# Spreading the last batch finishes, moving the table scatter, and a reordered opening in a fused attention and top-1 MoE kernel

## The chip, the core and the metric

The kernel runs on one core of a Trainium2 chip. The metric is the device time of one execution in microseconds. The engines are TensorE (PE, with its weight loads as PEld), VectorE (DVE), ScalarE (ACT), GpSimd (POOL) and SyncE (SP), which here only issues DMAs. DMAs are issued from SP's queue and, where an index list is needed, from POOL's.

## What is computed

Eight batches of block-causal attention (8 heads, 576 tokens, 64 columns per head), whose output x goes through a top-1 mixture of 8 experts:

```
scores = scale * q @ k.T            # masked where block(i) < block(j), block = 64 tokens
attn   = softmax(scores);  x = attn @ v          # x: 4608 rows of 512
logits = x @ w_gate;  e = argmax(logits);  gate_w = softmax(logits)[e]
eom    = sigmoid(x @ w_output_gate)
out    = gate_w * eom[e] * (relu(x @ w1[e]) @ w2[e])      # for the rows of each expert
```

## The kernel before

**Attention.** The work is done in 32 pairs of heads, p = 0 to 31, four pairs per batch. A pair has 8 turns: `PLAN` (line 310) is a list of names, a `|` ends a turn. S0 to S4 are the score matmuls of five query tiles, M the maxima on DVE, E the exponentials on ACT, F and C the transposes of the probabilities (PE) and their copies out of PSUM (ACT), V and X the product with v of an earlier pair. So a pair's scores, its transposes and its product lie in three consecutive pairs, and two pairs (p = 32 and 33) follow the last scores. From p = 1 to 31 the orders of PE, DVE and ACT are those of the program; POOL's and SP's orders are a planner's, which follows the program's priorities. Pair 0 has a list of its own, `OPENING`, and there only PE's order is the program's.

**Loads.** `Load` (lines 85 to 121) brings k and q of four heads (one unit, two pairs): `split` makes an fp16 high part and a low part, in eight pieces for a unit; on POOL the pieces are paced by ACT (`behind`); `turn` issues the DMA transposes on SP, and `swap` on DVE copies the transposed k with its halves exchanged. `load_heads` (line 126) puts the eight pieces on eight successive turns, then the transposes and swaps. `load_start` (line 149) is the opening: the first unit in two halves, transposed by PE against an identity, and the second unit.

**Finish of a batch.** `finish_steps` (line 515) returns a list of steps, one for each turn, from the second pair of the following batch: logits, their transposes and scaling, `heads` (the sum over the heads), `choose` (the expert), `ranks`, `own`, `slots`, `shares`, `gather`, `gate`, `weights`, `scatter`, and for each of five row tiles a transpose T (PE) and a store K (DVE, then a DMA to `x_d`). `pace` selects the list: 1 has 32 steps (batches 0 to 4), 2 has 16 (batches 5 and 6), 3 has 12 (batch 7, behind the attention). With pace 1 `heads` and two small products run on POOL, else on DVE. The scatter is five indirect DMAs on POOL's queue, one per row tile.

**Experts.** At p = 28 `load_first` (line 923) chooses the fullest expert by the counts of batches 0 to 5, fetches the ids and x rows of the first tiles (POOL's queue, behind all scatters so far), loads that expert's w1 and w2 and splits them on POOL: `split_slowly` one quarter of a chunk per turn, then w2. `first_tiles` (line 1167) transposes those x rows on PE from p = 33 on. After batch 7's finish `route_rest` (line 747) works out the table of tiles on DVE, and the rest of the expert stage follows; there PE multiplies the tiles in the order of `run` (line 1213).

The list for pace 1, with the scatter in the thirty-first of 32 places:

```
[lge], [ke, lgb], [kb, recips], [turn_logits], [scale_logits], [turn_last], [scale_last], [heads],
[], [], [T(0)], [K(0)], [], [choose], [], [],
[], [T(1), ranks], [own, K(1), T(2)], [K(2)], [T(3), slots], [shares], [K(3)], [],
[], [], [T(4)], [K(4)], [gather], [gate], [weights, scatter], [],
```

Of the kernel before, what the change touches and what calls it, by code (L numbers as in the profile page):

```python
# [27 lines left out]
def block_attention_top1_moe(  # L28
# [120 lines left out]
    def load_start():  # L149
# [15 lines left out]
        def halves(i, which, hi, lo):  # L165
            nat, sp = nats[which][:, i], sps[which][:, i]
            hi(sp[:, :, 0, :], nat)
            lo.tensor_tensor(sp[:, :, 1, :], nat, sp[:, :, 0, :], ALU.subtract)

        halves(0, 0, nc.vector.tensor_copy, nc.vector)  # L170
        halves(0, 1, nc.scalar.copy, nc.vector)
        rest = ps_t.tile([P, 512], F32, name="ps_t").rearrange("p (a n) -> p a n", n=P)
        for i, (sp, tr) in enumerate(((sps[0], kT), (sps[1], qT), (sps[0], sw))):
            sp = sp[:, 0]
            tv = tr[:, 0:half].rearrange("c (r p) -> c r p", r=nr)
            ps = ps_s.tile([P, 2, 512], F32, name="ps_s").rearrange("p a (b n) -> p (a b) n", n=P)
            for r in range(nr):
                o = ps[:, r] if r < 8 else rest[:, i]
                if i == 2:
                    for c in range(2):  # L180
                        nc.tensor.matmul(o[64 * c:64 * c + 64], sp[:, r, 1 - c, :], ident16, start=True, stop=True)
                else:
                    nc.tensor.matmul(o, sp[:, r].rearrange("p c d -> p (c d)"), ident16, start=True, stop=True)
            nc.vector.tensor_copy(tv[:, 0:4], ps[:, 0:4])
            nc.scalar.copy(tv[:, 4:8], ps[:, 4:8])
            nc.vector.tensor_copy(tv[:, 8], rest[:, i])
        loaded[0] = (qT, kT, sw)
        for which in range(2):
            halves(1, which, nc.scalar.copy, nc.gpsimd)
# [5 lines left out]
        def turned(groups):  # L195
            for grp in groups:
                ps = ps_t.tile([P, 512], F32, name="ps_t").rearrange("p (a n) -> p a n", n=P)
                for i, (m, r) in enumerate(grp):
                    sp = sps[1 if m == 1 else 0][:, 1]
                    if m == 2:  # L200
                        for c in range(2):
                            nc.tensor.matmul(ps[64 * c:64 * c + 64, i], sp[:, r, 1 - c, :], ident16, start=True, stop=True)
                    else:
                        nc.tensor.matmul(ps[:, i], sp[:, r].rearrange("p c d -> p (c d)"), ident16, start=True, stop=True)
                i = 0
                while i < len(grp):
                    m, r = grp[i]
                    n = sum(1 for mm, _ in grp if mm == m)
                    tr = trs[m][:, half:] if m == 2 else trs[m][:, nr:].rearrange("c r p -> c (r p)")
                    nc.any.tensor_copy(tr.rearrange("c (r p) -> c r p", p=P)[:, r:r + n], ps[:, i:i + n])  # L210
# [5 lines left out]
        turned([[(2, r) for r in range(4)], [(m, 8) for m in range(3)]])  # L216
        nxt.turn(0)
        yield
        turned([[(0, r) for r in range(4, 8)], [(1, r) for r in range(4, 8)]])
        yield  # L220
        turned([[(2, r) for r in range(4, 8)]])
        with tc.issue_after(last_max[0].ins):
            nxt.split(1, nc.vector.tensor_copy, nc.gpsimd)
# [8 lines left out]

    with tc.high_priority(offset=3000):
# [4 lines left out]

        mrow = const.tile([P, P], BF16, name="mrow")
# [26 lines left out]
        nc.vector.tensor_copy(tcol, t_i)  # L266
        nc.vector.tensor_scalar(erev, ecol, -1.0, float(E), ALU.mult, ALU.add)

        nc.vector.tensor_tensor(
            upto, ecol.unsqueeze(2).broadcast_to([P, E, E]), ecol.unsqueeze(1).broadcast_to([P, E, E]), ALU.is_ge  # L270
        )

        nc.vector.tensor_scalar(t64, tcol, 64.0, None, ALU.mult)

# [20 lines left out]
    def constants():  # L295

# [218 lines left out]
    def finish_steps(b, sums, xT, pace):  # L515
# [16 lines left out]
        eng = nc.gpsimd if pace == 1 else nc.vector  # L532
# [95 lines left out]

        def slots():
            rank = small.tile([P, NT], F32, name="rank")  # L630
            nc.vector.tensor_reduce(rank, rk, AX.X, ALU.add)
            add = small.tile([P, E], F32, name="add")
            nc.vector.tensor_reduce(add, oh.rearrange("p t e -> p e t"), AX.X, ALU.add)
            nc.vector.tensor_tensor(run_cnt[:, b + 1], run_cnt[:, b], add, ALU.add)
# [288 lines left out]
    def load_first():  # L923
# [23 lines left out]
        for r in range(5):  # L947
            yield
# [348 lines left out]
```

## Time and profile before

| what | us |
|---|---|
| median of 3 runs | 763.81 (761.55 to 764.34) |
| the profiled execution | 760.33 |
| its span, first to last instruction | 758.4 |
| PE busy in the span | 724.5 |
| ACT busy | 532.1 |
| DVE busy | 525.5 |
| POOL busy | 341.5 |

The times in the rows below are microseconds from the start of the span. A row of a timeline gives start, duration, engine, line, operation, output and inputs, how many instructions it stands for, and in brackets the idle time of the engine ahead of it with what ended it. The attention lies from about 10 to 358 us, the expert stage behind it.

### The profile page before, as it was taken

What the parts mean: (1) busy time and instruction counts of PE and PEld (TensorE: products, weight loads), DVE (VectorE), ACT (ScalarE), POOL (GpSimd) and SP (SyncE); (2) the same over time, 40 slices, a digit from 0 to 9 for tenths busy, and PEclk for the clock granted to TensorE, in tenths of its full rate; (3) what the DMA queues carried; (4) which work ended last, traced back from release to release, by engine and by line L of the source; (5) the groups of instructions that cost most, each with busy time, mean ns of one, the idle gap of its engine ahead of it and who ended that gap; (6) DMA issues with size and microseconds to landing.
All of it is one profiled execution on the core that took longest, in us unless ns stands there. A gap on an engine that the chain in (4) does not pass through costs nothing.

```text
span 758.4 us, 18741 instructions
## 1 busy us (share of the span) xinstructions
PE 724.5 (96%) x6918; PEld 510.5 (67%) x6918; DVE 525.5 (69%) x1058; ACT 532.1 (70%) x1193; POOL 341.5 (45%) x481
## 2 busy tenths in 40 slices
PE   5899999999999998889998999999999999999996
PEld 3677776767676665666866759667586676686662
DVE  6766776767776779676747958578587685895540
ACT  4999887988888886867117758577576675876531
POOL 6664647474757557396448423232222333301111
PEclk9999999999999999999999999999999999999999
DMA  8899877979696976862167997999999978741611
GB/s 153 175 207 189 178 168 151 203 131 218 123 217 105 214 151 138 198 183 78 64 222 214 290 308 198 290 272 377 294 299 328 302 208 287 222 78 43 240 41 45
DMA packets 256629, 147.87 MB, mean 195 GB/s; under 512 B 224144, under 2 KB 224208, under 8 KB 256528
## 3 DMA queue, kind: packets, MB, share of 16 engines
q1 hardware_dynamic: 248416, 127.30, 67.0%
q0 software_dynamic: 8112, 19.29, 7.8%
q8 instruction: 56, 0.92, 0.6%
q14 instruction: 45, 0.37, 0.2%
HBM read 126.03 MB, written 19.34 MB: 192 GB/s over the span
## 4 chain that ended last, share of the span: by engine, by line
PE 69%; DVE 10%; DMA 7%; ACT 7%; issue 4%; POOL 2%; POOLq 1%; SPq 0%; DVEq 0%; ACTq 0%
PE ps_s L1024 23%; PE ps_t L1053 19%; PE ps_t L456 7%; PE ps_a L491 5%; ACT pt L422 4%; DMA tr<-sp 4%; PE ps_s L390 3%; PE ps_s L391 3%; POOL tab_d L658 2%; PE ps_t L499 1%; PE ps_t L561 1%; ACT pT L1110 1%; DVE nmx L407 1%; PE ps_s L399 1%; PE ps_a L1077 1%
## 5 line engine op out<-in xcount | busy, mean ns | idle before, releaser
L1024 PEld LDWEIGHTS <-w1b 128*128 128x128 f16 (+1 forms) x2208 | 176.1, 98 | 26.1 <-DVE w1b L894 2.7
L1024 PE MATMUL ps_s<-xt,w1b 128*128 128x256 f16 (+5 forms) x1920 | 175.5, 253 | 3.2 <-DMA xt<-xr 1.8
L422 ACT ACTIVATE pt<-ps_s,nbs 128x512 f32<-128x512 f32 (+4 forms) x282 | 155.8, 577 | 25.5 <-DVE nbs L415 24.0
L1053 PE MATMUL ps_t<-w2b,hh 128*128 128x512 f16 (+1 forms) x560 | 166.9, 379 | 0.0
L894 DVE TENSOR_TENSOR w2b<-w2f,w2b 128x1024 bf16<-128x1024 f32 x80 | 92.9, 1220 | 88.8 <-ACT w2b L892 88.8
L407 DVE TENSOR_REDUCE nmx<-ps_s 128x2 f32<-128x1024 f32 (+1 forms) x125 | 102.6, 821 | 45.3 <-PE ps_s L392 44.3
L1110 ACT COPY pT<-ps_t 128x512 f32<-128x512 f32 (+1 forms) x221 | 112.7, 565 | 15.4 <-PE ps_t L456 15.2
L1062 POOL DMA_INDIRECT out_dram<-ys,ids x38 | 48.9, 1288 | 155.2 <-ACT ys L1061 87.7
L456 PE MATMUL ps_t<-ident,pt 128*128 128x128 f32 x768 | 108.5, 277 | 5.2 <-ACT pT L1110 2.9
L1053 PE MATMUL ps_t<-w2b,hl 128*128 128x512 f16 x280 | 106.2, 379 | 0.0
L1061 ACT ACTIVATE ys<-ps_t,ids 128x512 f32<-128x512 f32 (+1 forms) x38 | 26.1, 686 | 113.6 <-PE ps_t L1053 91.5
L1053 PEld LDWEIGHTS <-hh 128*128 128x128 f16 x560 | 54.3, 98 | 61.5 <-issue 0.3
L456 PEld LDWEIGHTS ps_t<-ident,pt 128*128 128x128 f32 x768 | 84.4, 141 | 15.4 <-ACT lgT L555 5.9
L894 DVE TENSOR_TENSOR w1b<-w1f,w1b 128x1024 bf16<-128x1024 f32 x80 | 92.9, 1217 | 1.0 <-ACT w1b L892 0.9
L108 POOL TENSOR_TENSOR sp<-nat,sp 128x320 f16<-128x320 f32 x120 | 89.5, 757 | 8.7 <-DVE sp L105 2.8
L105 POOL CAST sp<-nat 128x320 f16<-128x320 f32 x112 | 49.1, 453 | 82.5 <-ACT pT L1110 77.0
L892 ACT CAST w1b<-w1f 128x1024 f16<-128x1024 f32 x80 | 78.4, 1045 | 3.3 <-DMA w1f<-in_moe_w_dram 3.3
L892 ACT CAST w2b<-w2f 128x1024 f16<-128x1024 f32 x80 | 77.8, 1043 | 1.5 <-DMA w2f<-in_moe_w_dram 1.5
L390 PE MATMUL ps_s<-tr,tr 128*128 128x512 f16 (+1 forms) x250 | 71.8, 303 | 6.5 <-ACT pt L422 6.0
L491 PE MATMUL ps_a<-pT,va 128*64 128x384 f32 (+2 forms) x256 | 74.0, 412 | 0.0
L491 PE MATMUL ps_a<-pT,vb 128*64 128x384 f32 (+2 forms) x256 | 74.0, 412 | 0.0
L391 PE MATMUL ps_s<-sw,tr 128*128 128x512 f16 (+1 forms) x250 | 69.8, 302 | 0.0
(222 smaller groups left out, 1176.0 us busy)
## 6 DMA issues: line engine op xcount, KB each, us to landing
w1f<-in_moe_w_dram SPq DMA_DIRECT2D x80, 512.0 KB
w2f<-in_moe_w_dram SPq DMA_DIRECT2D x80, 512.0 KB
nat<-in_k_dram SPq DMA_DIRECT2D x15, 576.0 KB
nat<-in_q_dram SPq DMA_DIRECT2D x15, 576.0 KB
x_d<-xn SPq DMA_DIRECT2D x32, 256.0 KB
va<-in_v_dram SPq DMA_DIRECT2D x32, 128.0 KB
vb<-in_v_dram SPq DMA_DIRECT2D x32, 128.0 KB
hh<-in_moe_w_dram SPq DMA_DIRECT2D x4, 512.0 KB
```

The lines of the kernel that those rows point to most:

```text
L108: last_lo[0] = lo.tensor_tensor(sp[:, sl, 1, :], self.nats[i][:, sl], sp[:, sl, 0, :], ALU.subtract)
L390: nc.tensor.matmul(o, qq, k1[ab][:, 0:n], start=True, stop=False)
L391: nc.tensor.matmul(o, qq, k2[ab][:, 0:n], start=False, stop=False)
L407: nc.vector.tensor_reduce(nmx[t], at[t], AX.X, ALU.max, negate=True)
L422: last_act[0] = nc.scalar.activation(probs[t][:, ab * n:(ab + 1) * n], at[t, ab], AF.Exp, bias=nbs[t][:, ab:ab + 1], scale=SCALE, accum_ou ...
L456: nc.tensor.transpose(held[i][:, P * j:P * j + P], probs[t][:, sl], ident)
L491: nc.tensor.matmul(pa[half, c0:512], vs[a][:, j, :], rows[:, a, j, c0 - P:512 - P], start=(j == 0), stop=(j == 3))
L892: nc.scalar.copy(hi, src)
L894: eng.tensor_tensor(lo[at], src[at], hi[at], ALU.subtract)
L1024: nc.tensor.matmul(ph[:, f4].rearrange("p (h n) -> p h n", n=w), wv[:, cc, f, :], xv[:, cc], start=(k == 0), stop=(k == 3 * KD - 1))
L1053: nc.tensor.matmul(py, hv[:, f, h], wv[:, f, :], start=(k == 0), stop=(k == 3 * KF - 1))
L1110: last_act[0] = nc.scalar.copy(to, of)
```

## The change

The scatter of pace 1 moves from the thirty-first place of the list to the thirty-sixth, and each of its DMAs is issued behind the last low part of a split. Batch 5 gets pace 1, and pace 2 (batch 6 alone) gets 22 entries and uses POOL for `heads`. The counts of a batch are added in a step of their own, `tally`. In `load_first` the fetch of ids and x moves behind the third chunk of w1. The memsets of xg are paced by ACT. In the opening a partition holds four rows of a load that follow each other in DRAM, in two DMAs per load; a matmul then turns every fourth column, and the copy out of PSUM puts them in order by a read with a step of 128 elements; the blocks get PSUM buffers of their own, the split is divided into rows 0 to 4 and 5 to 8 over three engines, each copy has its engine named, and ACT's and DVE's orders are the program's. The second unit's split runs on POOL alone. Four constant operations move to pair 1.

```diff
-                nc.sync.dma_start(
-                    nat[:, i], src[0, 2 * i:2 * i + 2].rearrange("h s d -> (h s) d").rearrange("(n p) d -> p n d", p=P),
-                )
...
-        halves(0, 0, nc.vector.tensor_copy, nc.vector)
-        halves(0, 1, nc.scalar.copy, nc.vector)
...
+                rows = src[0, 2 * i:2 * i + 2].rearrange("h s d -> (h s) d")
+                nc.sync.dma_start(nat[:, i, 0:8].rearrange("p (a n) d -> p a n d", a=2), rows[0:8 * P].rearrange("(a p n) d -> p a n d", a=2, n=4))
+                nc.sync.dma_start(nat[:, i, 8], rows[8 * P:])
...
+        def keep(copy, m, i, r0, ps):
+            to = into(m, i, r0, r0 + (4 if r0 < 8 else 1))
+            if r0 < 8:
+                to, ps = to.rearrange("p (n j) -> p n j", j=4), ps.rearrange("p (j n) -> p n j", j=4)
+            copy(to, ps)
...
+        for which in range(2):
+            hi(0, which, (nc.vector, nc.scalar)[which], 0, 5)
+            hi(0, which, (nc.scalar, nc.vector)[which], 5)
+            lo(0, which, nc.vector, 0, 5)
+            lo(0, which, nc.gpsimd, 5)
...
+        keep(on_v, 0, 0, 0, kk[:, 0])
+        keep(on_v, 0, 0, 4, kk[:, 1])
+        keep(on_v, 0, 0, 8, last)
+        hi(1, 0, nc.scalar)
+        turn(2, 0, ss[0])
+        keep(on_v, 2, 0, 0, ss[0])
+        for r0, ps in ((0, qq[:, 0]), (4, qq[:, 1]), (8, rest[:, 0:P])):
+            turn(1, r0, ps)
+        keep(on_s, 1, 0, 0, qq[:, 0])
+        keep(on_s, 1, 0, 4, qq[:, 1])
+        turn(2, 4, ss[1])
+        turn(2, 8, rest[:, P:2 * P])
+        keep(on_v, 1, 0, 8, rest[:, 0:P])
+        keep(on_v, 2, 0, 8, rest[:, P:2 * P])
+        keep(on_s, 2, 0, 4, ss[1])
+        hi(1, 1, nc.scalar)
...
-        turned([[(0, r) for r in range(4)], [(1, r) for r in range(4)]])
-        nxt.split(0, nc.vector.tensor_copy, nc.gpsimd)
+        turned((on_s, [(0, r) for r in range(4)]), (on_v, [(1, r) for r in range(4)]))
+        with tc.issue_after(done.ins):
+            nxt.split(0, nc.gpsimd.tensor_copy, nc.gpsimd)
...
-    with tc.manual_schedule(engines={mybir.EngineType.PE}), tc.high_priority(offset=2000):
+    with tc.manual_schedule(engines=ORDERED), tc.high_priority(offset=2000):
         start = load_start()
...
-        eng = nc.gpsimd if pace == 1 else nc.vector
+        eng = nc.gpsimd if pace < 3 else nc.vector
...
+        def tally():
+            add = small.tile([P, E], F32, name="add")
+            nc.vector.tensor_reduce(add, oh.rearrange("p t e -> p e t"), AX.X, ALU.add)
+            nc.vector.tensor_tensor(run_cnt[:, b + 1], run_cnt[:, b], add, ALU.add)
...
-                sc = nc.gpsimd.indirect_dma_start(
+                with tc.issue_after(last_lo[0].ins):
+                    sc = nc.gpsimd.indirect_dma_start(
...
             return [
-                [lge, lgb], [ke], [recips], [], [heads, T(0)], [K(0), choose], [], [T(1)],
-                [K(1), ranks], [own, T(2)], [K(2), slots, shares], [T(3), gather], [K(3), gate], [T(4), weights], [K(4), scatter], [],
+                [lge], [ke, lgb], [recips], [], [heads], [T(0)], [K(0)], [],
+                [], [], [], [], [], [choose], [], [tally, T(1)],
+                [ranks, K(1)], [own, T(2)], [K(2), slots, shares], [T(3), gather], [K(3), gate], [T(4), weights], [K(4), scatter], [],
             ]
...
-            [], [], [T(0)], [K(0)], [], [choose], [], [],
+            [], [], [T(0)], [K(0)], [], [choose], [], [tally],
             [], [T(1), ranks], [own, K(1), T(2)], [K(2)], [T(3), slots], [shares], [K(3)], [],
-            [], [], [T(4)], [K(4)], [gather], [gate], [weights, scatter], [],
+            [], [], [T(4)], [K(4)], [gather], [gate], [weights], [],
+            [], [], [], [scatter],
...
-        fetch_ids(steps[0])
-        fetch_ids(steps[1], (0, 1))
-        fetch_x(steps[0])
-        fetch_x(steps[1], (0, 1))
...
             load(w2, c)
+            if c == 2:
+                fetch_ids(steps[0])
+                fetch_ids(steps[1], (0, 1))
+                fetch_x(steps[0])
+                fetch_x(steps[1], (0, 1))
...
-            later.append(finish_batch(*done, 1 if done[0] < B - 3 else 2 if done[0] < B - 1 else 3))
+            later.append(finish_batch(*done, 1 if done[0] < B - 2 else 2 if done[0] < B - 1 else 3))
...
-                nc.gpsimd.memset(xg[j], 0.0)
+                behind(nc.gpsimd.memset(xg[j], 0.0))
```

## Rows read from the trace of the kernel before

**Rows 1.** Stages: busy us of PE, PEld, DVE, ACT, POOL with counts; clock, DMA.
```profile
20.00:40.00 20.00, 16.73 (x170) 12.38 (x168) 13.39 (x38) 19.19 (x59) 13.16 (x23) 1.00 0.87 172
250.00:350.00 100.00, 90.98 (x955) 64.90 (x954) 77.05 (x227) 77.86 (x242) 61.02 (x101) 1.00 0.73 172
380.00:400.00 20.00, 20.00 (x181) 12.69 (x179) 8.02 (x41) 3.73 (x6) 9.84 (x11) 1.00 0.69 249
```

**Rows 2.** Line 399 on PE, four windows: durations, then first and last start.
```profile
L399 PE MATMUL ps_s<-tr,tr x16: 192/286/380, 65.4 to 97.2; 128*64 128x512 f16 x8, 128*64 128x64 f16 x8
...
L399 PE MATMUL ps_s<-tr,tr x16: 191/284/404, 106.3 to 139.8; 128*64 128x512 f16 x8, 128*64 128x64 f16 x8
...
L399 PE MATMUL ps_s<-tr,tr x16: 190/284/404, 273.2 to 312.3; 128*64 128x512 f16 x8, 128*64 128x64 f16 x8
...
L399 PE MATMUL ps_s<-tr,tr x12: 192/286/380, 321.4 to 346.9; 128*64 128x512 f16 x6, 128*64 128x64 f16 x6
```

**Rows 3.** PE's waits from 280 to 350 us: total, times, longest.
```profile
PE ps_t L456 <- ACT pT L1110: 2.9, 2, 1.6
PE ps_t L456 <- DVE xn L566: 2.0, 3, 1.3
```

**Rows 4.** Timeline: the sum over heads, on DVE (pace 2) and POOL (pace 1).
```profile
284.74 2.28 DVE L597 TENSOR_TENSOR lh<-lh 128x320 f32<-128x320 f32 x2
...
245.41 1.47 POOL L597 TENSOR_TENSOR lh<-lh 128x320 f32<-128x320 f32 x2
```

**Rows 5.** POOL around a scatter; DVE's waits at line 117: total, times, longest.
```profile
234.19 1.02 POOL L658 DMA_INDIRECT tab_d<-idg,sli  x1 [0.90 <-DVE idg L652]
...
240.25 0.74 POOL L105 CAST sp<-nat 128x192 f16<-128x192 f32 x2
...
DVE sw L117 <- DMA tr<-sp: 7.5, 4, 2.5
```

**Rows 6.** Timeline of the opening, by engine.
```profile
7.07 0.19 DVE L266 CAST tcol<-t_i 128x72 f32<-128x72 int32 x1
...
7.69 0.68 DVE L184 CAST tr<-ps_s 128x512 f16<-128x512 f32 x1
...
9.62 1.07 PE L181 MATMUL ps_s<-ident,sp 128*64 128x128 f16 x16 [0.73 <-ACT tr L185]
...
11.46 0.37 PE L391 MATMUL ps_t<-sw,tr 128*128 128x256 f16 x1 [0.35 <-DVE sw L184]
...
11.44 0.58 ACT L185 CAST sw<-ps_s 128x512 f16<-128x512 f32 x1 [1.39 <-DVE sw L184]
...
13.98 0.48 ACT L422 ACTIVATE pt<-ps_t,nbs 128x256 f32<-128x256 f32 x1
```

**Rows 7.** DMA rate in 40 slices: 0 to 20 us, then 500 to 520.
```profile
GB/s 0 0 0 0 180 252 286 282 209 213 230 223 219 215 219 217 219 217 219 216 219 219 216 219 217 222 253 65 0 0 0 0 0 0 0 144 211 215 216 219
...
GB/s 344 373 401 347 202 289 313 115 4 9 314 262 393 377 442 393 328 189 221 328 303 303 328 369 352 385 418 393 401 397 418 418 393 414 401 397 414 337 173 49
```

**Rows 8.** Timeline of DVE: a reduction read with a step, and one without.
```profile
377.21 1.19 DVE L766 TENSOR_REDUCE pt<-pt 128x32 f32<-128x576 f32 x1
...
290.48 0.74 DVE L411 TENSOR_REDUCE nmx<-ps_s 128x1 f32<-128x576 f32 x1
```

**Rows 9.** Timeline of POOL from first fetch to last scatter; one row of PE.
```profile
315.14 0.76 POOL L853 DMA_DIRECT2D ids<-tab_d  x1 [7.08 <-DMA tr<-sp]
...
324.48 0.41 POOL L898 CAST w1b<-hh 128x256 f16<-128x256 f32 x1
324.98 0.66 POOL L899 TENSOR_TENSOR w1b<-hh,w1b 128x256 bf16<-128x256 f32 x1
...
360.70 2.54 POOL L894 TENSOR_TENSOR w2b<-hl,w2b 128x256 bf16<-128x256 f32 x4
370.88 0.97 POOL L658 DMA_INDIRECT tab_d<-idg,sli  x1 [7.64 <-DVE sli L637]
...
354.67 1.09 PE L971 MATMUL ps_t<-ident,xg 128*128 128x128 f32 x8
```

More of the change, by code (lines that the diff above doesn't have):

```diff
@@ L172, in load_start @@
[L172 to L186, printed above, removed]
+                rows = src[0, 2 * i:2 * i + 2].rearrange("h s d -> (h s) d")
@@ new lines, in across, with into @@
+        def across(o, m, i, r):
+            sp = sps[1 if m == 1 else 0][:, i]
+            if m == 2:
+                for c in range(2):
+                    nc.tensor.matmul(o[64 * c:64 * c + 64], sp[:, r, 1 - c, :], ident16, start=True, stop=True)
+            else:
+                nc.tensor.matmul(o, sp[:, r].rearrange("p c d -> p (c d)"), ident16, start=True, stop=True)
+        def into(m, i, r0, r1):
+            tr = trs[m] if m == 2 else trs[m].rearrange("c r p -> c (r p)")
+            return tr[:, i * half + P * r0:i * half + P * r1]
@@ new lines, in turn @@
+        def turn(m, r0, ps):
+            for r in range(r0, min(r0 + 4, nr)):
+                across(ps[:, P * (r - r0):P * (r - r0) + P], m, 0, r)
+        on_v, on_s = nc.vector.tensor_copy, nc.scalar.copy
+        kk, qq = (ps_s.tile([P, 2, 512], F32, name="ps_s") for i in range(2))
+        ss = [bank() for i in range(2)]
+        rest = bank()
+        last = ps_a.tile([P, 512], F32, name="ps_a")[:, 0:P]
+        for r0, ps in ((0, kk[:, 0]), (4, kk[:, 1]), (8, last)):
+            turn(0, r0, ps)
@@ L187, in load_start @@
+        keep(on_s, 2, 0, 4, ss[1])
+        hi(1, 1, nc.scalar)
         loaded[0] = (qT, kT, sw)
         for which in range(2):
-            halves(1, which, nc.scalar.copy, nc.gpsimd)
+            done = lo(1, which, nc.gpsimd)
         nxt = Load(1)
@@ L192, in load_start, with turned @@
         yield
-        def turned(groups):
-            for grp in groups:
-                ps = ps_t.tile([P, 512], F32, name="ps_t").rearrange("p (a n) -> p a n", n=P)
+        def turned(*groups):
+            for copy, grp in groups:
+                ps = bank()
                 for i, (m, r) in enumerate(grp):
[L199 to L204, printed above, removed]
+                    across(ps[:, P * i:P * i + P], m, 1, r)
                 i = 0
@@ L208, in turned @@
                     n = sum(1 for mm, _ in grp if mm == m)
[L209 to L210 removed]
+                    keep(copy, m, 1, r, ps[:, P * i:P * (i + n)])
                     i += n
[L213 to L214 removed]
+        turned((on_s, [(0, r) for r in range(4)]), (on_v, [(1, r) for r in range(4)]))
+        with tc.issue_after(done.ins):
+            nxt.split(0, nc.gpsimd.tensor_copy, nc.gpsimd)
         yield
[L216 removed]
+        turned((on_s, [(2, r) for r in range(4)]), (on_s, [(m, 8) for m in range(3)]))
         nxt.turn(0)
         yield
[L219 removed]
+        turned((on_v, [(0, r) for r in range(4, 8)]), (on_s, [(1, r) for r in range(4, 8)]))
         yield
[L221 to L223 removed]
+        turned((on_s, [(2, r) for r in range(4, 8)]))
+        nxt.split(1, nc.gpsimd.tensor_copy, nc.gpsimd)
         yield
@@ L237, in block_attention_top1_moe @@
         make_identity(nc, ident)
+        warm = const.tile([P, 1], F32, name="warm")
+        nc.vector.memset(warm, 0.0)
+        nc.scalar.copy(warm, warm)
         mrow = const.tile([P, P], BF16, name="mrow")
@@ L674, in finish_steps @@
                 [lge], [ke, lgb], [kb, recips], [turn_logits, turn_last], [scale_logits, scale_last, heads, T(0)], [K(0), choose],
-                [ranks], [own, T(1)], [slots, shares, K(1), T(2)], [gather, K(2), gate, T(3)], [weights, scatter, K(3), T(4)], [K(4)],
+                [ranks], [own, T(1)], [tally, slots, shares, K(1), T(2)], [gather, K(2), gate, T(3)], [weights, scatter, K(3), T(4)], [K(4)],
             ]
```

35 lines of the change are left out of this document (18 added, 17 removed).

## The prediction

> **What bounds the kernel now.** I read the stage table first. TensorE (PE) has work in nearly all of the span, but between 250 and 350 us it is busy for only 91.0 us of 100 [rows 1]. Those 9.0 us are the largest hole there is. Next I read the pair clock: the first score matmul of a pair's last query tile (L399), one window for each group of four pairs [rows 2]. A group that carries the finish of one batch takes 106.3 - 65.4 = 40.9 us at best. The five groups with the slow finish (pace 1) take 273.2 - 65.4 = 207.8 us, which is 3.3 more than five times 40.9. The group from 273.2 to 321.4, in which batch 5 is finished at pace 2, takes 48.2 us, 7.3 more than 40.9. The wait table names the holes: between 280 and 350 us PE waits 2.9 us for ScalarE's (ACT) copies of turned probabilities and 2.0 us for VectorE's (DVE) stores of x [rows 3]. The ends of these waits lie in DVE's queue: at pace 2 the sum over heads stands there for 2.28 us, and the store that frees PE's bank comes only behind it in program order; on POOL the same two instructions took 1.47 [rows 4]. The last view is POOL's order: a scatter's five indirect DMAs run from 234.19 to 240.25, 6.06 us, and the split of the next heads goes on only behind them; DVE waits four times, 7.5 us in all and 2.5 at the longest, for the transposed heads that come from that split [rows 5]. From 380 to 400 us PE is full [rows 1], and the routing waits only for batch 7. So time won in the attention should reach the end one for one.
>
> **The change part by part.** I make the sum against the profiled execution, 760.33 us (span 758.4, 1.9 around it), which is 3.5 below the median 763.81.
>
> **Opening.** The chain to the first exponential at 13.98 is: k and q landed and split; five small constant operations on DVE from 7.07 to 7.69; copies; a PE wait of 0.73 for a bank that ACT frees (9.62); a wait of 0.35 for the copy of sw (11.46); the maxima [rows 6]. Four rows per partition make 1 KB runs of eight ninths of each load. The 256-byte runs of the opening move about 218 GB/s, the larger runs of the expert stage up to about 400 [rows 7]. A load of 295 KB takes 1.35 us at the first rate; as an estimate from the two rows, 0.9 at 330 GB/s. Two loads lie ahead of q: 0.9 earlier. The constants leave the chain: 0.62. Every transposed block has its own bank: 0.73, and the 0.35 behind it goes too, as sw is then copied earlier. That is 2.6 to the first exponential. From there ACT is nearly always busy (19.19 of 20 us from 20 to 40 [rows 1]), so ACT's own extra work counts: by the named engines it gets about one copy of 512 columns more than now, 0.6 by the 0.58 of L185 [rows 6]. Then the gapped reads: twelve copies take each next element from 512 bytes further on in PSUM. No row shows such a read. The bounds are nothing (the copies of today, 0.68 [rows 6]) and 1.6 times: a reduction over 576 elements with a step took 1.19, one without 0.74 [rows 8], so 0.4 more for each. Seven of them lie on the chain or on ACT, 0 to 2.8; a gain is excluded, as the same elements are read. I take 0.5, near the plain copy, since that reads PSUM as these do, and the stepped row reads SBUF. Opening: 2.6 - 0.6 - 0.5 = 1.5, with ends -0.8 and 2.6.
>
> The page SBUF — State Buffer of the Trainium skill, section "Door 1: The DMA port swizzle", speaks against these reads: PSUM delivers lines of 8 bytes, and an access that goes to a new line each time pays. It gives no price for DVE or ACT; no row of this case shows it for PSUM.
>
> The eight hi casts of the second load move to POOL, which is busy 13 of 20 us there [rows 1]: nothing, unless the transposes for pair 2 then come late; they wait behind the opening's last lo there, and behind them on POOL stands nothing that pair 0 or 1 reads. The memsets of xg leave POOL's opening queue, the constants go to pair 1, the tally is made earlier and the warm copy stands where ACT is idle: nothing for each, as DVE and POOL have idle time at the new places.
>
> **Scatter five places later (batches 0 to 4).** It now falls behind the last split piece of the load, not into its middle, so the transposes start about 6 us sooner and DVE's waits for them go. Bounds: 0, and the whole excess of 3.3. I take 2.3, because part of the excess are short waits for exponentials that have no scatter near them. What is late next: the sum over heads of the following batch, queued behind the scatter on POOL; its reader comes six turns later, so it is covered.
>
> **Batch 5 at pace 1.** Its steps go from two pairs to four and a half, and its heads to POOL. By the pair clock this would give 7.3. One wait stays: the heads of the last unit are loaded early; their transposes must wait until pair 27's last scores have freed the buffer (`sb` keeps two), and this is where DVE stands still longest, 2.5 us [rows 5]. I leave 1.2 of it in. And on POOL the scatter of batch 4 now stands ahead of all pieces of that load, and the heads of batch 5 among them, so DVE's choice of the expert may wait: another 1.1. Gain 7.3 - 1.2 - 1.1 = 5.0, ends 3 and 6.5.
>
> **Batch 6 over three pairs.** Its four groups of x transposes go from pairs 30 and 31 to the pair after the last scores. That is work of PE in either place and gives nothing. What goes are the stalls of pair 31, about 2.0 of the waits in [rows 3]. In the new place the turns are shorter, and some stall comes back: I take 1.5, ends 0 and 2.5.
>
> **POOL near the end.** The ids and x of the first tiles are fetched some 23 turns later, in the middle of the w1 split. Now: ids at 315.14, x until 324.48, and the w1 split waits behind it; w2 is split until 363.24, and POOL has 7.64 us free before the last scatter at 370.88 [rows 9]. Afterwards POOL must do, from pair 29's middle to the turn of the first x (PE at 354.67 now, about 343 then): 12 quarters of w1 by 0.41 and 0.66, 12.8; a scatter, 6.1; heads, 1.8 as an estimate (1.47 of [rows 4] and a third, smaller addition); the fetch with its waits, 9.3 (315.14 to 324.48); in sum 30.0 of about 36.5 us. With the landing some 3.5 us are left. Then 4.3 of w1, 10.2 of w2 (four times the 2.54) and 6.1 of scatter end near 357, and the last scatter is wanted at about 359. It fits, barely. I take a cost of 1.0, ends 0 and 4.
>
> Sum: 1.5 + 2.3 + 5.0 + 1.5 - 1.0 = 9.3, so 751.0 for an execution like the profiled one, and **754.5** against the median 763.81.
>
> **The rivals.** (a) *POOL late at the end*: the fetch stands behind more of the split than I count and PE waits at the first x transposes. For it: POOL is in order and its slack is 3.5 us. Against: it stands idle for 7.08 us ahead of the fetch now [rows 9], which the w1 split can use once the fetch is gone. Price 4 instead of 1: 757.5. (b) *Batch 5 still stalls*: the buffer wait and POOL's backlog persist and the pairs 27 and 28 keep most of their excess; the term gives 1.5 instead of 5.0: 758.0. (c) *The gapped reads cost 1.6 times*: the exposed 2.8 instead of 0.5: 756.8. (The rule of the Trainium skill's SBUF page, above, is this case.) (d) *All terms near their upper ends*: a gain of 14: 749.8. (e) *Slower*: POOL's planner puts the w2 split (10.2) and batch 6's scatter (6.1) ahead of the fetch of the first x. Decisive from the point where POOL's lateness passes 3.5 us: 16.3 - 3.5 = 12.8 lost at the first x transposes, ahead of batch 7's finish in PE's order, and the gain is gone: 754.5 - 1.0 + 12.8 = 766.3. Against: the planner kept the program's order of fetch, split and scatter in the trace.
>
> **How the numbers follow.** Forecast 0.50 (own range 751.5 to 758), (a) 0.14, (b) 0.10, (c) 0.10, (d) 0.08, (e) 0.08. The range leaves out most of (e) and the far ends of (a) with (b) together: 749 to 761. A measurement of this kernel tells 0.5% (3.8 us) from no change: faster means below 760.0, slower above 767.6. The forecast, (c) and (d) lie below 760.0, (a) and (b) for the most part: 0.79. Between: the rest of (a) and (b), and half of (e): 0.16. Slower: 0.05.
>
> **What would show it.** First exponential near 11.4 instead of 13.98. The copies out of PSUM at 0.68 (DVE) and 0.58 (ACT), or 1.0. No scatter between two pieces of a load's split, and DVE's wait for transposed heads down to about 2 us. The pair clock 41 to 42 from pair 25 to pair 29. POOL's fetch ending ahead of the first x transposes, with no PE wait there. Wrong would be: a group of four pairs still near 48, a PE wait for xg, or a later last scatter relative to its slot numbers.

## The result: 0.5% slower, and the profile after

The kernel after takes 765.7 us (763.3 to 768.42, 20 runs), the kernel before 761.62 in the same comparison: ratio 1.0052, 95% interval 1.0041 to 1.0064. The forecast was 754.5, range 749 to 761, made against a median of 763.81 for the kernel before, so 9.3 us of gain. It was wrong, in sign too. In the profiled execution (767.37, span 765.7) PE is busy for 728.9 us, ACT 534.8, DVE 522.7, POOL 352.2.

The stage tables say where. Columns: the stretch, its length, then busy us (and instructions) of PE, PEld, DVE, ACT and POOL, PE's granted clock, the DMA share and GB/s. The stretches run from the first score matmul of the last query tile of pair 5 to that of pair 25, from there to that of pair 31, and from there to the first expert matmul. First the kernel after (with the 100 us of [rows 1], where PE now has 13.4 us of hole instead of 9.0), then the kernel before as it was run again (e13 below), then the best kernel that the experiments found (e15).

```profile
250.00:350.00 100.00, 86.63 (x891) 62.24 (x887) 67.53 (x189) 73.02 (x226) 61.05 (x104) 0.93 0.62 141
...
62.30:269.70 207.40, 204.23 (x2181) 146.83 (x2178) 154.68 (x437) 182.05 (x559) 126.33 (x211) 1.00 0.92 177
269.70:337.40 67.70, 64.71 (x659) 46.15 (x656) 50.05 (x137) 54.65 (x170) 41.57 (x69) 0.95 0.60 133
337.40:366.10 28.70, 17.70 (x184) 12.87 (x181) 11.68 (x35) 10.21 (x23) 23.55 (x40) 0.76 0.31 99
```
```profile
65.20:274.50 209.30, 204.32 (x2181) 146.86 (x2177) 154.12 (x437) 180.45 (x559) 124.62 (x211) 1.00 0.87 173
274.50:349.40 74.90, 66.14 (x679) 46.51 (x675) 55.45 (x167) 54.89 (x172) 47.31 (x78) 0.98 0.65 158
349.40:363.00 13.60, 13.47 (x166) 9.08 (x160) 7.20 (x17) 9.75 (x21) 11.78 (x16) 1.00 0.16 46
```
```profile
61.60:266.60 205.00, 203.27 (x2179) 146.71 (x2175) 153.52 (x437) 181.36 (x559) 126.41 (x211) 1.00 1.00 179
266.60:335.10 68.50, 63.84 (x659) 45.33 (x657) 48.50 (x148) 54.76 (x170) 49.81 (x80) 0.98 0.69 154
335.10:350.90 15.80, 15.12 (x184) 10.64 (x181) 11.34 (x35) 9.90 (x23) 11.11 (x17) 1.00 0.26 91
```

The attention up to pair 31 became faster, about as forecast: pair 31's tile comes at 337.4, against 346.4 in the profile of before, 9.0 sooner, where the terms ahead of that point had summed to 10.3. That the two are near is partly luck: the opening gave more than forecast, pairs 5 to 25 almost nothing (207.8 to 207.4), and 2.1 us of it is work of batch 6 that only moved behind pair 31. These 9.0 and 6 us more go in the last stretch, 28.7 us long instead of 13.6 (13.7 in the first profile of before): PE is busy for 17.7 of it, at a clock of 0.76. Of its 184 matmul rows 18 more than before are batch 6's, moved there; with the same 184, e15 needs 15.8.

The pair clock, as [rows 2], L435 after for L399 before:
```profile
L435 PE MATMUL ps_s<-tr,tr x16: 192/286/379, 62.3 to 95.3; 128*64 128x512 f16 x8, 128*64 128x64 f16 x8
L435 PE MATMUL ps_s<-tr,tr x16: 192/286/379, 104.3 to 136.7; 128*64 128x512 f16 x8, 128*64 128x64 f16 x8
...
L435 PE MATMUL ps_s<-tr,tr x16: 192/285/403, 269.7 to 307.5; 128*64 128x512 f16 x8, 128*64 128x64 f16 x8
L435 PE MATMUL ps_s<-tr,tr x12: 191/284/403, 316.5 to 337.9; 128*64 128x512 f16 x6, 128*64 128x64 f16 x6
```
The waits from 280 to 370 us (engine, line, waited for: total, times, longest), as [rows 3]:
```profile
POOL w1b L939 <- ACT pT L1152: 15.9, 1, 15.9
ACT d L678 <- POOL d L647: 11.5, 1, 11.5
...
PE ps_t L597 <- ACT xT L1152: 10.8, 1, 10.8
DVE zs L683 <- POOL z L646: 10.2, 1, 10.2
```
Four waits of 10 to 16 us, each once, in place of [rows 3]'s short ones. The first lies ahead of the others: POOL stands idle for 15.88 us up to 313.99, because the program paces the w1 split by ACT. The timelines show how the other three hang together; POOL from 313 us on, as [rows 9], then the end of the same split in the kernel before:
```profile
313.99 0.40 POOL L939 CAST w1b<-hh 128x256 f16<-128x256 f32 x1 [15.88 <-ACT pT L1152]
...
318.75 1.04 POOL L697 DMA_INDIRECT tab_d<-idg,sli  x1 [1.43 <-DVE idg L690]
...
327.74 0.90 POOL L697 DMA_INDIRECT tab_d<-idg,sli  x1 [0.30 <-issue]
...
333.98 0.77 POOL L894 DMA_DIRECT2D ids<-tab_d  x1 [4.18 <-DMA tab_d<-idg,sli]
...
342.83 1.03 POOL L905 DMA_INDIRECT xg<-x_d,ids  x1 [0.17 <-issue]
...
349.66 0.67 POOL L940 TENSOR_TENSOR w1b<-hl,w1b 128x256 bf16<-128x256 f32 x1
350.28 0.25 POOL L647 TENSOR_TENSOR d<-L,mx 128x40 f32<-128x40 f32 x1
350.50 0.26 POOL L646 TENSOR_TENSOR z<-L,oh 128x40 f32<-128x40 f32 x1
```
```profile
343.25 0.67 POOL L899 TENSOR_TENSOR w1b<-hl,w1b 128x256 bf16<-128x256 f32 x1
```
and ACT, DVE and PE behind it in the kernel after, with the stage row of the 13 us in which the clock is low:
```profile
350.57 0.24 ACT L678 ACTIVATE d<-d 128x40 f32<-128x40 f32 x1 [11.53 <-POOL d L647]
...
350.79 0.20 DVE L683 TENSOR_REDUCE zs<-z 128x5 f32<-128x40 f32 x1 [10.17 <-POOL z L646]
...
338.62 0.66 PE L597 MATMUL ps_t<-ident,xT 128*128 128x128 f32 x4
...
350.96 1.12 PE L597 MATMUL ps_t<-ident,xT 128*128 128x128 f32 x4 [10.75 <-ACT xT L1152]
...
343.00:356.00 13.00, 5.04 (x24) 4.35 (x26) 4.40 (x18) 5.32 (x11) 9.63 (x20) 0.50 0.46 153
```
Two products of 0.25 us on 128x40 elements stand last in POOL's queue behind the whole w1 split, with batch 5's scatter and the fetch inside it. ACT and DVE, which run in program order, stand at the readers of these products; pair 31's last exponential and the copies out of PSUM are queued behind them, so PE stands 10.75 us and then runs at half clock (the transposes of one tile take 1.12 us, just before 0.66). The split ends at 350.33, 12.9 us behind pair 31's tile; in the kernel before it ended at 343.92, 2.5 us ahead of that tile.

### The profile page after: what moved, and what is told of

It reads as the page before. It is cut to its first block, busy times and chain, and to the rows that moved or that the text cites. A ratio compares the mean times of both kernels' runs of the same rounds, so it can differ in the third digit from the quotient of the medians.

```text
span 765.7 us, 18754 instructions
## 1 busy us (share of the span) xinstructions
PE 728.9 (95%) x6918; PEld 515.0 (67%) x6918; DVE 522.7 (68%) x1041; ACT 534.8 (70%) x1196; POOL 352.2 (46%) x501
## 4 chain that ended last, share of the span: by engine, by line
PE 75%; DVE 6%; DMA 5%; ACT 5%; POOL 4%; issue 3%; POOLq 1%; SPq 0%; DVEq 0%; ACTq 0%
PE ps_s L1066 23%; PE ps_t L1095 19%; PE ps_t L492 9%; PE ps_a L527 7%; PE ps_s L426 4%; PE ps_s L427 3%; ACT pt L458 2%; PE ps_t L535 2%; ACT pT L1152 2%; PE ps_t L597 2%; PE ps_s L435 2%; PE ps_a L526 1%; PE ps_a L1119 1%; PE ps_t L585 1%; DMA out_dram<-ys,ids 1%
## 5 line engine op out<-in xcount | busy, mean ns | idle before, releaser
L458 ACT ACTIVATE pt<-ps_s,nbs 128x512 f32<-128x512 f32 (+4 forms) x282 | 155.1, 571 | 15.9 <-DVE nbs L451 13.6
L492 PE MATMUL ps_t<-ident,pt 128*128 128x128 f32 x768 | 111.6, 282 | 1.5 <-DVE xn L602 0.9
L1103 ACT ACTIVATE ys<-ps_t,ids 128x512 f32<-128x512 f32 (+1 forms) x38 | 26.1, 686 | 112.2 <-PE ps_t L1095 95.7
L492 PEld LDWEIGHTS ps_t<-ident,pt 128*128 128x128 f32 x768 | 87.2, 144 | 11.5 <-ACT lgT L591 5.9
L105 POOL CAST sp<-nat 128x320 f16<-128x320 f32 x120 | 53.0, 457 | 82.8 <-ACT pT L1152 71.6
L527 PE MATMUL ps_a<-pT,va 128*64 128x384 f32 (+2 forms) x256 | 74.2, 413 | 0.0
L527 PE MATMUL ps_a<-pT,vb 128*64 128x384 f32 (+2 forms) x256 | 74.2, 413 | 0.0
```

The source lines that it names most:

```text
L458: last_act[0] = nc.scalar.activation(probs[t][:, ab * n:(ab + 1) * n], at[t, ab], AF.Exp, bias=nbs[t][:, ab:ab + 1], scale=SCALE, accum_ou ...
L492: nc.tensor.transpose(held[i][:, P * j:P * j + P], probs[t][:, sl], ident)
L527: nc.tensor.matmul(pa[half, c0:512], vs[a][:, j, :], rows[:, a, j, c0 - P:512 - P], start=(j == 0), stop=(j == 3))
```

## The experiments

Each ratio is against the kernel before on the same chip: e1 to e4 on one chip (before 764.87), e5 to e8 on a second (775.64), e9 to e12 on a third (775.87), e13 to e16 on a fourth (764.87), e17 and e18 on a fifth (777.33). On the three chips with the long times, every kernel traced there takes 12.4 to 14.3 us from pair 10 to 11 and for each fourth pair after it, 9.6 being the best elsewhere (stretch 5 to 25: 218.6 to 221.7); why stays open below; compare runs of one chip, and the last column everywhere. All kernels traced on those three have the later scatter; the kernel before has no trace there. The ratios are those on record, which are not the quotients of the medians (e4: 757.80 by 764.87 is 0.991); e4 and e15 have four runs each, e14 seven, e2 eight, the others ten. The stretches are differences of times read to 0.1 us.

| run | ratio (95%) | pair 5 to 25 | 25 to 31 | 31 to first expert matmul |
|---|---|---|---|---|
| e1 products of batch 6 on DVE | 0.9980 (0.9957 to 1.0003) | 207.5 | 65.8 | 25.1 |
| e2 batch 6 all on DVE | 0.9954 (0.9921 to 0.9987) | 207.4 | 65.9 | 25.7 |
| e3 opening alone | 0.9979 (0.9948 to 1.0009) | 210.2 | 74.9 | 13.6 |
| e4 scatter alone | 0.9866 (0.9826 to 0.9907) | 205.2 | 70.7 | 13.7 |
| e5 after, batch 6 as before | 1.0007 (0.9979 to 1.0035) | 221.4 | 69.5 | 22.4 |
| e6 scatter and batch 5 | 1.0058 (1.0029 to 1.0087) | 219.5 | 69.5 | 22.4 |
| e7 scatter and opening | 1.0013 (0.9985 to 1.0042) | 220.4 | 74.2 | 19.7 |
| e8 after, POOL's order mended | 1.0045 (1.0018 to 1.0071) | 221.7 | 67.6 | 26.1 |
| e9 scatter alone | 1.0050 (1.0022 to 1.0078) | 220.6 | 74.9 | 19.5 |
| e10 scatter and opening | 1.0019 (0.9990 to 1.0048) | 218.6 | 74.1 | 19.9 |
| e11 scatter, batch 6 spread | 0.9976 (0.9947 to 1.0006) | 218.9 | 69.8 | 15.8 |
| e12 after, w2's casts later | 1.0018 (0.9991 to 1.0045) | 220.3 | 67.1 | 21.5 |
| e13 before itself | 0.9983 (0.9959 to 1.0008) | 209.3 | 74.9 | 13.6 |
| e14 after itself | 1.0060 (1.0034 to 1.0085) | 207.5 | 65.9 | 29.5 |
| e15 opening, scatter, batch 6 spread | 0.9866 (0.9830 to 0.9902) | 205.0 | 68.5 | 15.8 |
| e16 the same, scatter at its old place | 0.9973 (0.9944 to 1.0002) | 209.2 | 70.9 | 15.8 |
| e17 e15 and batch 6's sums on POOL | 0.9928 (0.9899 to 0.9957) | 219.9 | 69.1 | 15.6 |
| e18 e15 and the fetch moved | 0.9918 (0.9883 to 0.9954) | 220.1 | 68.7 | 15.8 |

**What holds ACT and DVE (e1, e2, e12).** Edits on the kernel after: e1 puts the two products on DVE for batch 6, e2 batch 6's sums as well, e12 is e2 with ACT's casts of w2 later.
```diff
-            eng.tensor_tensor(z, lz, oh, ALU.mult)
-            eng.tensor_tensor(d, lg, mxb, ALU.subtract)
+            few = nc.gpsimd if pace == 1 else nc.vector
+            few.tensor_tensor(z, lz, oh, ALU.mult)
+            few.tensor_tensor(d, lg, mxb, ALU.subtract)
...
-        eng = nc.gpsimd if pace < 3 else nc.vector
+        eng = nc.gpsimd if pace == 1 else nc.vector
...
-        for r in range(5):
+        for r in range(12):
             yield
         for c in range(4):
             with tc.issue_after(last_act[0].ins):
                 split_w2(nc.gpsimd, 0, wc[c], c)
```


> The changed kernel with one edit: the two small products z and d of batch 6 go back to DVE; its sum over heads stays on POOL. Theory 1 (POOL's queue): in the changed kernel PE stands still for 10.75 us because ACT and DVE, which work in program order, wait 11.5 and 10.2 us for d and z, and those stand on POOL behind the fetch and the w1 split. Then the PE wait near 340 us goes to under 2 us, the stretch of half clock behind it (13.65 us) goes too, and the time is 12 to 17 us below the changed kernel's 765.7: 749 to 754. Theory 2 (the spread itself: the x transposes of batch 6, moved behind the last scores, are what PE loses): the wait changes its name but not its length, and the time stays within 3 us of 765.7.

> The changed kernel with the engine choice undone as a whole: batch 6's sum over heads and both products on DVE. Theory 1: as the run with the products alone, 749 to 754, and DVE's wait of 1.17 us for the sum (at 338.3 us) goes, while the sum costs DVE 2.3 to 2.8 us one turn group earlier; so within 2 us of that run. If the sum over heads, not the products, were what holds the queue, this run would be far faster than that one (over 5 us). Theory 2: within 3 us of 765.7.

By their ratios both are faster than the kernel after, by 0.7 and 1.0%, but not by the 12 to 17 us of Theory 1: e1's 764.38 us lies in the band of Theory 2. The traces decide otherwise. ACT's wait for the products is 1.67 us in e1 instead of 11.53, as Theory 1 has it, and a second stall stands where the first had been: 4.86 us in e1, 7.36 in e2. ACT's timeline of e2:
```profile
340.23 1.05 ACT L933 CAST w2b<-hl 128x1024 f16<-128x1024 f32 x1
...
348.72 1.04 ACT L933 CAST w2b<-hh 128x1024 f16<-128x1024 f32 x1 [6.95 <-DMA hh<-in_moe_w_dram]
...
353.06 1.04 ACT L933 CAST w2b<-hl 128x1024 f16<-128x1024 f32 x1 [2.81 <-DMA hl<-in_moe_w_dram]
```
A chunk of w2 is loaded into the buffer of a chunk of w1, and so only when POOL has split that; ACT stands at the cast, and the copies of the last probabilities stand behind it. So the products alone return 3.0 (e2) to 3.6 us (e1) of the last stretch's 28.7, and the next thing in the way is the wait for w2.

> The kernel after with batch 6's sums and products on VectorE and ScalarE's casts of w2 seven turns later in its order. If the stall of 7.4 us is ScalarE standing at these casts for w2, which GpSimd's late w1 split holds back: no PE stall over 2 us between 335 and 362, no stretch of half clock there, first expert matmul 6 to 9 us sooner against pair 31 (17 to 20 us instead of 25.7), and the wait may come back as a wait of the first second-layer products for w2. If PE's stall has another cause (the products of batch 6, the x rows): it stays over 4 us.

With the casts later ACT's waits for w2 are gone and PE's longest stall between pair 31 and the expert stage is 1.77. The last stretch is 21.5 instead of 25.7, which is more than the 17 to 20 expected, and one stretch of half clock stays (356.1 to 359.5). So the wait for w2 is one route by which POOL's lateness reaches PE, the products are another; what holds the remaining 5.7 us against e15's 15.8 no run separates.

**Whose lateness it is (e5, e6, e8).** e5 is the kernel after with the old list for batch 6 and its sums on DVE. e6 is the kernel before with the later scatter, the tally apart, batch 5 at pace 1 and the fetch behind the third chunk of w1. e8 is e2 with the expert chosen two turns later, the w1 split earlier and the fetch later in the program.
```diff
-            later.append(finish_batch(*done, 1 if done[0] < B - 3 else 2 if done[0] < B - 1 else 3))
+            later.append(finish_batch(*done, 1 if done[0] < B - 2 else 2 if done[0] < B - 1 else 3))
```


> The kernel after, with batch 6 finished as in the kernel before (16 steps, sums on VectorE) and all else of the change kept. Theory A (spreading batch 6 into pair 32 is the loss: there its steps stand in VectorE's and ScalarE's order behind what is late): pair 31 starts near 343, from pair 31 to the first expert matmul 14 to 17 us as before, first expert matmul near 358, time some 758. Theory B (the loss is GpSimd's late w1 split, whatever batch 6 does: ScalarE's casts of w2 still stand behind it): from pair 31 to the first expert matmul 20 us or more, a PE stall of over 4 us between 345 and 360, time 762 or more.

> The kernel before, with the scatter five places later, the tally apart and batch 5 at pace 1 (the fetch of ids and x moved behind the third chunk of w1, as this needs), without the opening and without batch 6's spread. Compared with the scatter alone (757.8): my forecast's step for batch 5 says 5.0 less, 753. Rival b says 1.5 less or nothing (pair 25 to pair 29 still 46 to 47 us): 756 to 758. Theory B of the run before says slower than the scatter alone, near 762, with the loss behind pair 31.

> The kernel after with four places changed, batch 6 still spread: batch 6's sums on VectorE; the fullest expert chosen two turns later; the w1 split begun seven turns sooner against that, in GpSimd's idle time before 314; the fetch of ids and x behind the fourth chunk of w1 and three more turns before the w2 split. If GpSimd's lateness near the end is the whole loss (ScalarE's casts of w2 and the products of batch 6 waiting for it): no PE stall over 2 us between 335 and 360, from pair 31 to the first expert matmul 19 us or less (14 and the pair's own moved work), pair 27 to pair 28 near 12.5, time 752 to 755. If the spread itself is the loss: pair 31 to the first expert matmul still over 22, time 760 or more.

In e5 and e6 batch 6 is finished as before, and still the last stretch is 22.4, against 19.7 in e7 on that chip, which has batch 5 at its old pace. In e5 ACT waits 3.4 and 2.9 for w2, and PE 3.4 at the transposes of the x rows, for a copy that ACT makes behind that. The times in us that I had expected of e5 to e8 were set by the first chip and say nothing on this one, so I go by the stretches. Theory B holds in its direction: POOL is late without batch 6's new list, the w1 split ending 9.0 and 9.1 us behind pair 31's tile. But the stall is 3.4, not over 4, and since e7 has 19.7 on that chip the lateness costs 2.7 there; the larger loss needs batch 6's new list as well. Pace 1 for batch 5 shortens the stretch from 25 to 31 by 4.7 (74.2 in e7, 69.5 in e5) and returns 2.7 of that. e8 did not mend it. With the later choice w1's load was issued only 1.9 us ahead of pair 28's last tile (6.1 in the kernel after), and POOL, free for the split, stood 10.17 us for its landing, up to 324.32; the split ended 4.9 us behind pair 31's tile, and ACT again stood 4.31 at a cast of w2. No run starts the split sooner with the choice left at its place, although POOL is idle for 15.88 us ahead of it: the first piece of w1 landed 4.5 us behind its issue in e8, which would make it 305.6 in the kernel after, as an estimate, against a start at 313.99.

**Each part alone and again (e3, e4, e7, e9, e10, e11).**
```diff
-            [], [], [T(4)], [K(4)], [gather], [gate], [weights, scatter], [],
+            [], [], [T(4)], [K(4)], [gather], [gate], [weights], [],
+            [], [], [], [scatter],
```


> The kernel before with the new opening alone (loads, splits, named engines, gapped reads, constants in pair 1, memsets of xg paced). The trace of the changed kernel has pair 0's last tile 3.3 us earlier and pair 5's 3.1 earlier. Theory 1: this gain reaches the end, so 3 us below the kernel before (758.6 if that is 761.6), and the gapped copies take 0.68 us on DVE and 0.58 on ACT. Rival: the opening's gain is lost before the end, because the last units' loads or POOL set the end: within 1 us of the kernel before. My forecast's term was 1.5.

> The kernel before with the scatter of pace 1 five places later, behind the last low part of a split, and nothing else (batches 0 to 4). My forecast's term was 2.3 us of gain. The trace of the changed kernel gives less: from pair 5 to pair 25 it takes 207.4 us, against 207.8 before, though one stall of 0.9 us stands in it at 88.9. So by the trace a gain of 0 to 1.5 us, and no wait of DVE for transposed heads but the last unit's. If the scatter in its old place had cost what the chain of waits suggests, 2 to 3 us.

> The kernel before with the opening and the scatter five places later, nothing else. If the two gains add: pair 5 near 63.0 (2.5 sooner), pair 5 to pair 25 205.2 as with the scatter alone, time near 755.5. If the opening's gain is lost again at stalls later on, as it was without the scatter's move: the same time as with the scatter alone, 757.8, with pair 5 to pair 25 near 207.5.

> The kernel before with the scatter five places later and nothing else, run again beside the three that follow. If its 1.3% is the kernel's own and not that chip's: ratio 0.985 to 0.991 again, with pair 5 to pair 25 in 205 to 206 us where nothing else disturbs the chip. If it was an accident of that chip: ratio 0.995 or more.

> The kernel before with the opening and the later scatter, beside the scatter alone on the same chip. If the opening's 2 to 3 us stay: 0.2 to 0.4% under the scatter alone, pair 5 near 63 against 65.7 and the same distance still at pair 31. If they are lost at later stalls: no difference at pair 31.

> The kernel before with the later scatter and batch 6 finished over three pairs on VectorE; batch 5, the opening, and GpSimd's fetch and split of w1 as before, so GpSimd is early. If the spread is good as such and only GpSimd's lateness spoils it: pair 31 starts 4 us sooner than with the scatter alone, from pair 31 to the first expert matmul 13.7 grows by 2 to 3 us at most, time 1 to 2 us under the scatter alone. If the spread only moves the work: pair 31 4 us sooner and the first expert matmul at the same time or later, from pair 31 to it 18 us or more.

In e3 the opening brings pair 5 2.0 us sooner than in the profile of before, but by pair 25 that is gone: DVE stands 3.30 for the transposed heads behind a scatter at its old place, and PE 2.00 at 123.06 for the store of x behind that. e4 is worth 1.3% on its chip, more than the forecast gave it. e9, the same kernel, is 0.5% slower than before on the third chip. Its trace has a stall in the second pair of each finish, where PE, ACT and DVE stand together: PE 1.61 at 120.9 us, ACT 3.6 up to the same point. e13 fell on a chip without such stalls (pairs 10 to 11 and the next three of the kind: 11.2, 9.6, 9.6 and 10.2), so whether the kernel before has them too stays open, and with it why the scatter's gain is lost there. The opening's gain is small against the noise: 2.3 us for e10 against e9, 0.5 for e3 against the kernel before, with intervals that overlap in the one pair and include 1 in the other. e11 against e9 shows batch 6's spread as a gain when POOL is early: pair 31 sooner by 5.9, the first expert matmul by 9.6 us; part of that are e9's own stalls; on chips without them the spread leaves 0 to 1.8 us (below, batch 6).

**The change without batch 5's part (e13 to e18).** e15 is the kernel before with the opening, the later scatter and the 22 entries for batch 6 on DVE. e16 has the scatter at its old place. e17 adds batch 6's sums on POOL to e15, e18 the fetch's move.
```diff
-        eng = nc.gpsimd if pace == 1 else nc.vector
+        eng = nc.gpsimd if pace == 1 or b == B - 2 else nc.vector
```


> The kernel before, unchanged, for its trace beside the others of this call. If the stall in the second pair of each finish belongs to the chip: pair 10 to 11, 14 to 15, 18 to 19 and 22 to 23 take 12.5 to 14 us here too (10.5 and 9.6 in the trace of before). If it belongs to the scatter's new place: they take 9.6 to 10.5, and the time lost on such a chip lies elsewhere.

> The kernel after, unchanged, beside the others of this call. If the result is the same on every chip: ratio 1.004 to 1.007. The stall behind pair 31 (10.75 us in the trace of after) must be here again, whatever the chip: ScalarE and VectorE stand for GpSimd's two products of batch 6.

> The kernel before with the opening, the later scatter and batch 6 over three pairs on VectorE; batch 5 at its old pace, so GpSimd's fetch and w1 split stand where they stood. If GpSimd's lateness was the whole loss of the change: from pair 31 to the first expert matmul under 17 us, and a time 5 to 8 us under the kernel before (ratio 0.990 to 0.994). If the opening's gain is lost at later stalls as well: 2 to 3 us under it (0.996).

> The same with the scatter at its old place. Against e15 it prices the scatter's move with all else equal: 2.6 us slower in pair 5 to pair 25 if the first result for the scatter alone (205.2 against 207.8 us) holds on this chip, equal or faster if the second one does.

> Opening, later scatter and batch 6 over three pairs, batch 5 as before, and batch 6's sums and products on GpSimd as in the kernel after. If GpSimd is only harmful where it is late: it is not late here, no PE stall over 2 us behind pair 31, the same ratio as without this (0.983 to 0.990). If its place in the order is harmful as such: a stall of several us behind pair 31, with ScalarE and VectorE standing for the products.

> The same kernel with batch 6's sums on VectorE and the fetch of ids and x behind the third chunk of w1, as in the kernel after. If the fetch's place is the loss: ScalarE stands at the casts of w2 or PE at the x rows, from pair 31 to the first expert matmul 20 us or more, and ratio 0.995 or more. If it needs batch 5's scatter for that: w1's split ends by 340 us, from pair 31 to the first expert matmul 15 to 17 us, ratio 0.983 to 0.990.

e15 takes 753.78 us against 764.87 and on that chip beats both kernels, by more than was expected of it. e14 has the stall again, 10.78 us. In e17 the products lie on POOL as in the kernel after, and nobody stands for them, because the w1 split is through:
```profile
349.41 0.68 POOL L942 TENSOR_TENSOR w1b<-hl,w1b 128x256 bf16<-128x256 f32 x1
350.55 0.28 POOL L646 TENSOR_TENSOR d<-L,mx 128x40 f32<-128x40 f32 x1 [0.47 <-DVE mx L636]
351.61 0.26 POOL L645 TENSOR_TENSOR z<-L,oh 128x40 f32<-128x40 f32 x1 [0.79 <-DVE oh L644]
```
In e18 the fetch stands four places later in the program and yet ahead of the split on POOL, as in the kernel before:
```profile
322.88 0.76 POOL L896 DMA_DIRECT2D ids<-tab_d  x1 [5.83 <-DMA tr<-sp]
...
331.31 0.40 POOL L941 CAST w1b<-hh 128x256 f16<-128x256 f32 x1
```
So this run says nothing of a late fetch; its ratio, like e17's, lies between the two expected ranges, on a chip of the slower kind. It says that the edit of the fetch alone doesn't make it late: in the kernel after it also waits for batch 5's scatter, 4.18 us of that for the landing. What is left between e15 and the kernel after, beside the tally, is batch 5 at pace 1. The end of the w1 split sorts the traces by it: in each of the twelve with batch 5 at its old pace the split ends 0.6 to 4.1 us ahead of pair 31's tile, in each of the eight with batch 5 at pace 1 (all with the moved fetch) 4.9 to 13.6 us behind it. So batch 5 at pace 1, with the fetch that then waits for its scatter, makes POOL late; no run added it alone to e15.

## Why the prediction was wrong, step by step

**Opening, 1.5: right in mechanism, too small.** Pair 5's tile comes 3.1 sooner (65.4 to 62.3), above my upper end of 2.6; the opening alone (e3) gives 2.0, e16 beside e13 on one chip 3.8 (65.2 to 61.4). The first exponential starts at 10.55 instead of the forecast 11.4 [rows 6]:
```profile
5.92 1.28 DVE L188 CAST tr<-ps_s 128x512 f16<-128x512 f32 x2
...
8.45 0.60 ACT L188 CAST sw<-ps_t 128x512 f16<-128x512 f32 x1
...
10.55 0.47 ACT L458 ACTIVATE pt<-ps_t,nbs 128x256 f32<-128x256 f32 x1
```
The gapped copies of 512 columns take 0.68 to 0.69 each on DVE and 0.58 to 0.62 on ACT, where the plain ones took 0.68 to 0.69 and 0.58 to 0.59: rival (c) is out, and the 0.5 that I put in was nearly nothing. The Trainium skill's page SBUF — State Buffer, section "Door 1: The DMA port swizzle", gives PSUM lines of 8 bytes and says that a non-contiguous pattern there slows matmuls; at these reads by DVE and ACT, with a step of 512 bytes, the trace shows no such price.

**Scatter, 2.3: too small.** e15 against e16 gives 4.2 us in pairs 5 to 25 (209.2 to 205.0), above my upper end 3.3, and 7.4 in all (761.18 to 753.78), on that chip. There the kernel before has more to lose than in the profile that I read: 209.3 (e13) instead of 207.8, or 4.8 above five times 40.9. Nearly all of it goes, and I had taken short waits out of it. Another 2.6 goes in pairs 25 to 29 (50.1 to 47.5), where batch 4's scatter falls; I had left that out of this term. DVE's waits of [rows 5] for transposed heads, 7.5 us, are gone from the kernel after.

**The tally, nothing: wrong.** The kernel after has the same scatter and takes 207.4 for these pairs (207.5 in e14, on e15's chip), e15 205.0. For batches 0 to 4 the tally's own step is what only the kernel after has. It stands on DVE ahead of the maxima:
```profile
86.47 0.23 DVE L667 TENSOR_REDUCE add<-oh 128x8 f32<-128x40 f16 x1 [0.23 <-issue]
86.74 0.76 DVE L668 TENSOR_TENSOR run_cnt<-run_cnt,add 128x8 f16<-128x8 f16 x1
87.42 0.68 DVE L443 TENSOR_REDUCE nmx<-ps_s 128x2 f32<-128x512 f32 x1
```
In e15 DVE waits 0.24 for PE ahead of these maxima; here 0.99 of tally lies there, and PE stands 0.90 us at 88.9 for the store of x behind them. The four later groups lose 0.3 to 0.4 each at the same pair. My reason, that "DVE and POOL have idle time at the new places", was an average; this place had next to none.

**Batch 5 at pace 1, 5.0: half of it came.** From pair 25 to 29, all on one chip, the kernel before takes 50.1 (e13), e15 47.5 and the kernel after 45.0 (e14): 2.5 for what e14 has beyond e15, which is batch 5's pace with the tally, the fetch and batch 6's sums. The 7.3 that I gave to batch 5 held batch 4's scatter, 2.6 on that chip. And a wait that I did not name came in: the choice of the expert counts batches 0 to 5, so PE stands 2.65 at 293.6 for batch 5's counts.
```profile
296.22 0.17 PE L734 MATMUL ps_t<-run_cnt,ones 128*128 128x8 f16 x1 [2.65 <-DVE run_cnt L668]
```
In this execution PE then runs at 0.51 of the clock from 295 to 302, and pairs 25 to 29 take 46.8; in e14 the same stall, 2.64, leaves the clock at full. Rival (b) comes near the size (1.5) by another cause: DVE's wait for the last unit's buffer, which it names, is gone from the trace.

**Batch 6, 1.5: about right where POOL is early.** Its steps cost 15.8 - 13.7 = 2.1 behind pair 31 and bring 2.2 ahead of it (e4 to e15, two chips, 70.7 to 68.5): about nothing, as the work is PE's in either place. On one chip, with the scatter at its old place (e13 to e16, which has the opening too), they bring 4.0 and cost 2.2. In the kernel after they hang on POOL.

**POOL near the end, -1.0: the step that failed.** The sum was nearly right: 30.0 us of work from the first split at 313.99 would end at 344.0, and the last x row was fetched at 343.9. The start was not: 36.5 us up to 343 would begin at 306.5, and the split began 7.5 later, behind the 15.88 us in which POOL stood for ACT. That took more than the slack of 3.5. And the waiter was the wrong one. I measured POOL's lateness at the x transposes, wanted at about 343. But batch 6's two products were wanted from 339.0 (ACT) and 340.6 (DVE), where their last rows before the wait end, and came from 350.3 on, behind the rest of the w1 split; and w2's casts on ACT want the end of that split as well. ACT and DVE have the last pair's work behind these. The price: 28.7 against 15.8 us in e15, 12.9 in place of 1.0; of it 10.3 are PE's idle time (28.70 - 17.70 against 15.80 - 15.12) and 2.6 the half clock behind it. PE never waits for x rows in the kernel after. Rival (a) names the engine and the cause, with the wrong place and a price of 4. Rival (e) gave nearly the result, 766.3, but by an order that the trace doesn't show: w2's split and batch 6's scatter did not go ahead of the fetch.

## What to carry to other kernels

When work moves onto an engine with a queue of its own, sum the queue and then list every reader in an engine with a fixed order, with the time at which it wants its operand: the earliest of them sets the slack, not the largest transfer. A tiny operation of 0.25 us at the end of a queue of 36 us holds an ordered engine until the queue is through, here for 10 to 12 us. And a hole seen in the profile belongs to one cause only once the other edits are taken out of it: undo or do each part alone before gains are added.

## What the runs showed of the hardware

A PSUM read with a step of 512 bytes in the copies of 128x512 elements cost next to nothing over a plain one, on DVE (0.68 to 0.69, plain 0.68 to 0.69) and ACT (0.58 to 0.62, plain 0.58 to 0.59). In the profiled execution of the kernel after PE's granted clock fell to half (0.50, the lower of its two levels) during or behind the stalls of 2.65 and 10.75 us, and also behind one of 1.17 us at 9.9; from 343 to 356 us it was 0.50 on average. The length of a stall did not decide it: in e14, the same kernel, it stayed at full behind 2.64 us, and in the kernel before behind 1.57 at 338.2. The time differs between chips for the same program: the kernel before took 764.87 us on two of the chips and 775.6 to 777.3 on three, and the later scatter's gain of 1.3% on one of the former was a loss of 0.5% on one of the latter. What makes the difference is not settled.
